# Attention output made as column pairs in the gate/up stage instead of as single sets in the down stage

## The chip, the cores and the metric

The kernel runs on one core of one Trainium2 chip. The metric is the device time of one execution in microseconds; quoted is the median of several executions. Ratios are computed as the mean time of one kernel's fast runs over the mean of the other's fast runs of the same rounds, so they are not quite the ratio of the medians quoted beside them (nor, in the main comparison, quite that of the means of the four times listed for each kernel, which is 0.9993 where the record has 0.9989).

## The reference, cut to what matters

```python
xn = layernorm(x)                                  # x: 2048 x 1024
q, k, v = split(xn @ wqkv)                         # 32 heads of 32
pq, pk = phi(q), phi(k)
kv  = einsum("hsd,hse->hde", pk, v);  z = sum_s(pk)
o   = (pq @ kv) / (pq . z + 1e-6)                  # per head
s   = o @ wo
g   = silu( (silu(xn @ w_gate) * (xn @ w_up)) @ w_down )   # hidden width 3584
out = x + s * g
```

The kernel folds `kv` and `wo` into one 1024 x 1024 matrix M, so that `s` = (normalised pq) @ M. It works in two passes of 1024 rows. A pass has a gate/up stage (queries, gate and up projections, hidden blocks kept in SBUF) and a down stage (four column sets; each gives a quarter of the output columns).

## The kernel before: the parts that matter

Every large product is done with a seven-product scheme: a 2 x 2 block product takes 7 block products in place of 8, paid for with sums of blocks on VectorE. In gate/up two column sets form a **pair**, and products 1 and 5 of both sets, which share the moving operand, are done together by the same scheme once more with 256 columns (the *inner* scheme).

The operand order of TensorE is fixed; a planner in the kernel's own Python gives each other engine a fixed order too, by deadlines that it works out from TensorE's order. ScalarE and VectorE then run that order whatever happens.

After the queries of a pass are made, they are normalised. ScalarE scales the broadcast reciprocals by z, VectorE multiplies, and the result goes to DRAM:

```python
def normalise_part(p, j, half):           # four parts for each pass
    ...                                    # four broadcast loads of 128 KB into rb
    for gl in range(4):
        ...
        act([z_r, zrr], [zrr], zr, zr, ACT.Identity, "sb", scale=zc[:, g:g + 1])
        tt([sr, zrr], [sr], dst, src, zr, ALU.mult, True)
    dma([H.reg(o, 4 * KB)], [named("q", p, half, j)], q_scr[p, half, j], ...)
```

In the down stage the queries come back into X and each of the four sets does 14-matmul products D1 to D7 (down projection) and 4-matmul products S1 to S7 (attention), both with 512 columns:

```python
feed(None)
pq_load(p)                                 # 4 loads of 512 KB, then the four query combinations
for c in range(4):
    Sx = wd_load(c);  ms = m_load(c);  d_set(p, c, Sx, ms)
# inside d_set, by set:
seq = ("D1 D5 D6 D2 D7 S1 S5 D3 S2 S6 D4 S7 S3 S4", ...)[min(c, 2)]
xo_ring, pt_ring, t4_ring = rings[link]    # t4_ring: three places of 2 KB for the T4 differences
```

Product D4 needs seven differences T4 = R10 - T2, made by VectorE as they are used.

Of the kernel before, what the change touches and what calls it, by code (L numbers as in the profile page):

```python
# [10 lines left out]
ALU = mybir.AluOpType  # L11
# [209 lines left out]
def build_kernel(nc, A_x, A_wqkv, A_wo, B_w_gate, B_w_up, B_w_down, out, WINDOW=6, NWARM=14, NPE=4, LEAD=12.0):  # L221
# [12 lines left out]
    with ExitStack() as es:  # L234
# [44 lines left out]
        m_v = m_scr.rearrange("(g p) c -> p g c", p=128)  # L279
        q_scr = nc.dram_tensor("q_scratch", [2, 2, 2, 128, 4 * 512], FP16)  # L280
        r_scr = nc.dram_tensor("r_scratch", [2, 2, 32, 512], BF16)
# [134 lines left out]
        rr_ring = Ring(TM, 20 * KB, 2 * KB, 1)  # L416
        fin_ring = Ring(TM, 10 * KB, 1 * KB, 8)
        x_ring = Ring(W, 32 * KB, 2 * KB, 4)
# [21 lines left out]
        XV = [xview(0, X), xview(1, P)]  # L440
        QV = xview(0, X)

# [491 lines left out]

        def wload(src, joint):


            s = raw_ring.take()
            dma([], [s.r], s.ap().rearrange("p (kt n) -> p kt n", n=512), src, dsem("wr%d" % s.k), 1024 * KB)
            v = s.ap().rearrange("p (kt w n) -> p w kt n", w=2, n=256)  # L940
            c = cmb_ring.take()
# [38 lines left out]
        IN_AT = (((W, 48 * KB), (W, 49 * KB), (W, 50 * KB)), ((W, 51 * KB), (TM, 8 * KB), (TM, 9 * KB)))  # L980
        xin = {}

        def x_inner(v):

            for m, at in zip((1, 5), IN_AT):
                ap, r = v[XOF[m]]
                B = {(k, j): ap[:, 2 * k:2 * k + 2, 256 * j:256 * j + 256] for k in range(2) for j in range(2)}
                t = [(a.at(o, KB, FP16).rearrange("p (k t) -> p k t", t=256), a.reg(o, KB)) for a, o in at]
                tt([r], [t[1][1]], t[1][0], B[1, 1], B[0, 1], ALU.subtract, True)
                tt([r], [r], B[0, 1], B[0, 1], B[0, 0], ALU.subtract, True)  # L990
                tt([r], [t[0][1]], t[0][0], B[1, 1], B[0, 1], ALU.subtract, True)
                tt([r, t[0][1]], [t[2][1]], t[2][0], B[1, 0], t[0][0], ALU.subtract, True)
                xin[m] = {1: (B[0, 0], r), 2: (B[1, 0], r), 3: (B[1, 1], r), 5: (B[0, 1], r), 6: t[0], 7: t[1], 4: t[2]}

        def joint_of(jstat, s0, s1):
            def ops(m):
                def f(k):
                    ws, wr = jstat(m, k)
                    xa, xr = xin[m][k]
                    return [(ws[q], xa[:, q, :]) for q in range(2)], [wr, xr]  # L1000
                return f
            return {"1": Joint(ops(1), lambda w, b: (s0, s1)[w].put1(b)),
                    "5": Joint(ops(5), lambda w, b: (s0, s1)[w].put5(b))}
# [17 lines left out]
        def q_load(p, s):  # L1021
            return wload(wqkv_v[:, :, s * 512:(s + 1) * 512], QJ[p][s])

        PQ0 = 52 * KB

# [46 lines left out]

        RB0 = 68 * KB

        def normalise_part(p, j, half):
# [9 lines left out]
            for gl in range(4):  # L1085
# [5 lines left out]
                tt([sr, zrr], [sr], dst, src, zr, ALU.mult, True)  # L1091
            o = PQ0 + (2 * half + j) * 4 * KB
            dma([H.reg(o, 4 * KB)], [named("q", p, half, j)], q_scr[p, half, j], H.at(o, 4 * KB, FP16),
                dsem("pq%d%d" % (half, j)), 512 * KB)

# [56 lines left out]

        def pq_load(p):
            for j in range(2):
                for k in range(2):
                    v, vr = xblock(X, 2 * j + k)
                    dma([named("q", p, k, j)], [vr], v, q_scr[p, k, j].rearrange(
                        "p (g t) -> p g t", t=512), dsem("pql%d%d" % (k, j)), 512 * KB)
            combos(QV)


        GB = 3584

        rings = ((Ring(TM, 18 * KB, 2 * KB, 3), Ring(TM, 24 * KB, 1 * KB, 2),
                  Places([(W, 40 * KB), (W, 42 * KB), (TM, 8 * KB)], 2 * KB)),
                 (Ring(X, 8 * KB, 2 * KB, 3), Ring(X, 14 * KB, 1 * KB, 2),
                  Places([(W, 40 * KB), (W, 42 * KB)], 2 * KB)))
        dd_ring = Ring(TM, 4 * KB, 2 * KB, 2)
        MR, MC = 44 * KB, 48 * KB
        PL_A, PL_B, PL_C, PL_D, PL_E = 8 * KB, 24 * KB, 16 * KB, 32 * KB, 0  # L1170
        RAW_AT = ((PL_A, PL_B), (PL_E, PL_A), (PL_B, PL_E), (PL_A, PL_B))

        def wd_load(c):


            A = {}
            for k in range(2):
                o = RAW_AT[c][k]
                v = W.at(o, 2 * GB).rearrange("p (n q) -> p n q", q=256)
# [17 lines left out]

        def m_load(c):
            raw = W.at(MR, 4 * KB, FP16).rearrange("p (g n) -> p g n", n=256)
            rr = W.reg(MR, 4 * KB)  # L1200
            dma([named("mscr", c // 2)], [rr], raw, m_v[:, :, c * 256:(c + 1) * 256], dsem("mld"), 512 * KB)
            cv = W.at(MC, 4 * KB, FP16).rearrange("p (m kt n) -> p m kt n", m=4, n=128)
            cr = [W.reg(MC + q * KB, KB) for q in range(4)]
            A = {(k, i): raw[:, 4 * k:4 * k + 4, i * 128:i * 128 + 128] for k in range(2) for i in range(2)}
            tt([rr], [cr[0]], cv[:, 0], A[0, 1], A[1, 1], ALU.add, True)
            tt([rr, cr[0]], [cr[1]], cv[:, 1], cv[:, 0], A[0, 0], ALU.subtract, True)
            tt([rr], [cr[2]], cv[:, 2], A[0, 0], A[0, 1], ALU.subtract, True)
            tt([rr, cr[1]], [cr[3]], cv[:, 3], A[1, 0], cv[:, 1], ALU.subtract, True)

            def stat(w, m):  # L1210
                if m in (1, 2, 4):
                    k, i = {1: (0, 0), 2: (1, 0), 4: (1, 1)}[m]
                    return [raw[:, 4 * k + q, i * 128:i * 128 + 128] for q in range(4)], rr
                q4 = {5: 0, 6: 1, 7: 2, 3: 3}[m]
                return [cv[:, q4, q, :] for q in range(4)], cr[q4]
            return stat

        out_evs = []

        def d_set(p, c, Sx, mstat):  # L1220
            gv, sv, xo = {}, {}, {}
            last = (p, c) == (1, 3)
            link = (p, c) == (0, 3)
            xo_ring, pt_ring, t4_ring = rings[link]

            def fin(i, j):
                if (i, j) not in gv or (i, j) not in sv:
                    return
                g, s = gv[i, j], sv[i, j]
                tt([g.r, s.r], [g.r], g.ap(FP16), g.ap(FP16), s.ap(FP16), ALU.mult, True)  # L1230
                row = p * 1024 + j * 512
# [47 lines left out]
            def dops(m):  # L1279
# [17 lines left out]
                for q in range(0, NPAIR, 7):  # L1297
# [3 lines left out]
            dset = Set(dops, keep(gv, ACT.Silu), dd_ring)  # L1301
            sset = xset(mstat, 0, QV, keep(sv, ACT.Identity), dd_ring)
            seq = ("D1 D5 D6 D2 D7 S1 S5 D3 S2 S6 D4 S7 S3 S4", "D1 S1 D5 S5 S2 D6 S6 D2 S7 S3 D7 S4 D3 D4",
                   "S1 S5 S2 S6 D1 S7 S3 D5 S4 D6 D2 D7 D3 D4")[min(c, 2)]
            if link:
                seq = "S1 S5 S2 S6 D1 S7 S3 D5 S4 X D6 nj1a D2 nj1b D7 nj1c D3 nj1d nj5a D4 nj5b n2_0 nj5c n6_0 n2_1 nj5d n6_1"
                nxt = None
            for w in seq.split():
                if w == "X":
                    nxt = turn_pass()  # L1310
                elif w[0] == "n":
                    nxt.do(w[1:])
                else:
                    (dset if w[0] == "D" else sset).step(int(w[1]))
                    tick()
# [4 lines left out]
        combos(XV[0])  # L1320
        order = [("q", 0), ("g", 0), ("u", 0), ("q", 1)] + [(k, n) for n in range(1, NPAIR // 2) for k in "gu"]
        lq = deque([(k, p, n) for p in range(2) for k, n in order])
        got = {}
        gate = [0]

        def pump(n):
            while lq and len(got) < n and lq[0][1] <= gate[0]:
                k, p, s = lq.popleft()
                got[k, p, s] = q_load(p, s) if k == "q" else gu_load(k, s)

# [10 lines left out]
        def turn_pass():  # L1341
# [3 lines left out]
            gate[0] = 1  # L1345
            raw_ring.__init__([(W, o * KB) for o in (0, 16, 8)], 8 * KB)
            cmb_ring.__init__([(X, 0), (W, 24 * KB), (W, 32 * KB)], 8 * KB)
            in_ring.__init__([(W, o * KB) for o in (44, 46, 40, 42)], 2 * KB)
# [5 lines left out]
        for p in range(2):  # L1354
            for k, n in order:
# [8 lines left out]
                if n == 2:  # L1364
                    at = {w: [partial(normalise_part, p, "gu".index(k), h)] for h, w in enumerate(("2_1", "7_1"))}
                if last_pair[0] is not None and (p, k, n) == (1, "q", 0):
                    pass
                elif k == "q":
                    q_pair(p, n, st, at)
                else:  # L1370
                    gu_pair(p, k, n, st, at)
# [3 lines left out]
            feed(None)  # L1375
            pq_load(p)
            for c in range(4):
                Sx = wd_load(c)
                ms = m_load(c)
                d_set(p, c, Sx, ms)  # L1380
        flush()
# [68 lines left out]
```

## Time and profile before

| kernel before | value |
|---|---|
| time, median of 4 | 731.58 us (731.53 to 733.25) |
| TensorE busy, profiled execution | 717.3 of 731.5 us |
| VectorE, ScalarE busy | 596.5 us, 397.7 us |
| matmuls | 3894 |

The lines that carry this are in the prediction below.

For comparing traces I use one derived quantity, the **loss** of TensorE: for each matmul, the distance to the next start less what a matmul of its width takes undisturbed (215.7 ns at 512 columns, 109.2 ns at 256; the few other shapes with the distance that they usually show). The sum of the undisturbed distances is the ideal time.

### The profile page before, as it was taken

How to read it: one execution, taken by the hardware profiler on the slowest of the kernel's cores; microseconds unless marked ns; L12 is line 12 of the kernel's file. 1: busy time of each engine (PE TensorE's matmuls, PEld its weight loads, DVE VectorE, ACT ScalarE, POOL GpSimd, SP SyncE). 2: the span in 40 equal slices, each digit the busy share in tenths (PEclk: the TensorE clock that was granted, in tenths of full speed). 3: DMA queues.
4: the chain of work that ended last, by engine and by line, in shares of the span. 5: the costliest groups of instructions: out<-in, count | busy, mean ns of one | idle time of the engine just before them, and what ended most of it. 6: DMA issues, size and time to landing. Idle time of an engine off the chain costs nothing.

```text
span 731.5 us, 10526 instructions
## 1 busy us (share of the span) xinstructions
PE 717.3 (98%) x3894; PEld 365.9 (50%) x3894; DVE 596.5 (82%) x1395; ACT 397.7 (54%) x743; POOL 14.1 (2%) x35
## 2 busy tenths in 40 slices
PE   8999999999999999999999999999999999999996
PEld 3444445455555555544444455555455554444442
DVE  6999868979989998787457889999899988757353
ACT  3776654787659766623232376767786654223231
POOL 2111000000000000000000000000000000000000
PEclk9999999999999999999999999999999999999999
DMA  9443235135257432471846534132835245274822
GB/s 293 110 102 86 44 111 176 59 109 166 75 149 217 156 109 65 130 216 32 213 118 153 170 86 152 59 116 76 245 145 173 74 136 167 77 166 118 177 65 50
DMA packets 135219, 94.00 MB, mean 129 GB/s; under 512 B 32512, under 2 KB 131072, under 8 KB 135168
## 3 DMA queue, kind: packets, MB, share of 16 engines
q1 hardware_dynamic: 135168, 93.34, 44.9%
q8 instruction: 30, 0.49, 0.3%
q14 instruction: 21, 0.17, 0.1%
HBM read 75.50 MB, written 10.62 MB: 118 GB/s over the span
## 4 chain that ended last, share of the span: by engine, by line
PE 86%; DVE 6%; ACT 4%; DMA 2%; issue 1%; POOL 0%; SPq 0%; ACTq 0%; DVEq 0%
PE ps L210 86%; ACT TM L341 2%; ACT H L341 2%; DMA W<-in_B_w_up_dram 1%; DVE H L717 1%; DVE W L348 1%; DVE ps L348 1%; DVE stats L642 1%; DVE TM L348 1%; DVE H L348 1%; ACT L341 1%; DVE TM L716 0%; DVE stats L646 0%; DMA W<-in_A_x_dram 0%; ACT ps L341 0%
## 5 line engine op out<-in xcount | busy, mean ns | idle before, releaser
L210 PE MATMUL ps<-X,W 128*128 128x512 f16 (+1 forms) x1408 | 312.0, 361 | 0.9 <-DVE ps L348 0.5
L341 ACT ACTIVATE TM<-ps 128x512 f16<-128x512 f32 (+2 forms) x337 | 181.7, 556 | 152.6 <-PE ps L210 148.5
L210 PE MATMUL ps<-H,W 128*128 128x512 f16 (+1 forms) x896 | 206.8, 379 | 0.3 <-DVE ps L348 0.3
L210 PEld LDWEIGHTS ps<-X,W 128*128 128x128 f16 (+1 forms) x1408 | 136.6, 98 | 122.2 <-DVE ps L348 2.3
L348 DVE TENSOR_TENSOR W<-W 128x256 f16<-128x256 f16 (+6 forms) x424 | 169.1, 440 | 9.7 <-DMA W<-in_B_w_down_dram 5.7
L348 DVE TENSOR_TENSOR ps<-ps,TM 128x256 f32<-128x256 f32 (+1 forms) x218 | 117.1, 540 | 33.1 <-PE ps L210 32.2
L210 PEld LDWEIGHTS ps<-H,W 128*128 128x128 f16 (+1 forms) x896 | 87.2, 98 | 103.4 <-DVE ps L348 0.7
L341 ACT ACTIVATE ps<-ps 128x512 f32<-128x512 f32 (+1 forms) x156 | 78.6, 504 | 59.3 <-PE ps L210 55.6
L341 ACT ACTIVATE H<-ps 128x512 f16<-128x512 f32 (+1 forms) x126 | 74.9, 602 | 57.4 <-PE ps L210 57.2
L210 PE MATMUL ps<-P,W 128*128 128x256 f16 (+1 forms) x440 | 90.0, 323 | 0.1
L210 PE MATMUL ps<-W 128*128 128x256 f16 (+1 forms) x328 | 69.7, 299 | 2.2 <-DVE ps L348 1.7
L348 DVE TENSOR_TENSOR TM<-ps,TM 128x512 f32<-128x512 f32 (+1 forms) x60 | 40.8, 681 | 29.4 <-PE ps L210 28.8
L341 ACT ACTIVATE TM<-TM 128x512 f16<-128x512 f32 (+1 forms) x61 | 37.9, 621 | 44.1 <-DVE TM L348 43.6
L210 PEld LDWEIGHTS ps<-P,W 128*128 128x128 f16 (+1 forms) x440 | 42.9, 98 | 32.9 <-DVE H L717 0.5
L348 DVE TENSOR_TENSOR H<-H,TM 128x512 f16<-128x512 f16 x112 | 45.2, 417 | 12.7 <-ACT H L341 12.4
L348 DVE TENSOR_TENSOR H<-H 128x1024 f16<-128x1024 f16 (+2 forms) x82 | 50.5, 629 | 0.6 <-DMA H<-in_A_wqkv_dram 0.3
L210 PEld LDWEIGHTS ps<-W 128*128 128x128 f16 (+1 forms) x328 | 30.8, 98 | 27.9 <-DVE ps L348 3.5
L348 DVE TENSOR_TENSOR TM<-TM 128x512 f16<-128x512 f16 (+1 forms) x59 | 24.2, 419 | 18.3 <-DMA TM<-TM 10.7
L210 PE MATMUL ps<-H,X 128*128 128x512 bf16 (+1 forms) x136 | 32.2, 379 | 1.2 <-ACT X L341 0.8
L210 PE MATMUL ps<-TM,W 128*128 128x256 f16 (+1 forms) x144 | 30.9, 296 | 0.3 <-DVE ps L348 0.3
L348 DVE TENSOR_TENSOR W<-H 128x1024 f16<-128x1024 f16 x40 | 26.9, 685 | 3.0 <-PE ps L210 2.8
L716 DVE TENSOR_SCALAR TM<-TM 128x512 f16<-128x512 f16 x64 | 17.7, 285 | 10.3 <-ACT TM L341 10.1
(81 smaller groups left out, 413.1 us busy)
## 6 DMA issues: line engine op xcount, KB each, us to landing
W<-in_B_w_gate_dram SPq DMA_DIRECT2D x14, 1024.0 KB, 5.3
W<-in_B_w_up_dram SPq DMA_DIRECT2D x14, 1024.0 KB, 5.5
W<-in_B_w_down_dram SPq DMA_DIRECT2D x16, 896.0 KB, 6.1
W<-in_A_x_dram SPq DMA_DIRECT2D x16, 256.0 KB, 3.0
H<-in_A_wqkv_dram SPq DMA_DIRECT2D x8, 512.0 KB, 8.3
W<-in_A_wqkv_dram SPq DMA_DIRECT2D x4, 1024.0 KB, 5.2
H<-r_scratch SPq DMA_DIRECT2D x32, 128.0 KB, 4.0
q_scratch<-H SPq DMA_DIRECT2D x8, 512.0 KB, 4.0
```

Of the source, the lines that this page charges most:

```text
L210: last = h.matmul(o, l, r, start=st, stop=sp, skip_group_check=True)
L341: return PL.op("act", reads, writes, lambda h: h.activation(o, i, func, **kw), nel(o) / 1200.0 + (0.055 if src == "ps" else 0.095))
L348: return dve(reads, writes, lambda h: h.tensor_tensor(o, a, b, op), nel(o), 1.92 if fast else 0.96)
L642: o0 = dve([s.r], [sA], lambda h: h.bn_stats(stats[:, j, 0, :], xa[:, 0:512]), 512)
L716: dve([e.r], [b.r], lambda h: h.tensor_scalar(ba, ea, 1.0, EPS_PHI, ALU.min, ALU.add), 512, 2.6)
L717: dve([src_r, b.r], [out_r], lambda h: h.scalar_tensor_tensor(out_ap, src, 0.0, ba, ALU.max, ALU.add), 512)
```

## The change

The attention output of a pass is made in the gate/up stage, after the eighth of the gate and up pairs, as two pairs in the style of the gate pairs (inner scheme included), straight from the queries in SBUF. The results wait in DRAM until the down stage multiplies them in. The down sets keep only D1 to D7. Memory places are dealt out anew, and in the second pass T4 gets eight places instead of three. The core of the diff, cuts marked:

```diff
-        q_scr = nc.dram_tensor("q_scratch", [2, 2, 2, 128, 4 * 512], FP16)
+        s_scr = nc.dram_tensor("s_scratch", [2, 4, 2, 128, 2 * 512], FP16)
 ...
-            o = PQ0 + (2 * half + j) * 4 * KB
-            dma([H.reg(o, 4 * KB)], [named("q", p, half, j)], q_scr[p, half, j], ...)
 ...
-        def pq_load(p): ...
+        def s_load(n):
+            return wload(m_v[:, :, n * 512:(n + 1) * 512], (1, 5), FP16, [named("mscr", n)])
+        def s_pair(p, n, stats, at):
+            def evac(w):
+                def f(i, j, ap, r, bank):
+                    o = st_ring.take()                       # four places of 1 KB
+                    act([r], [o.r], o.ap(FP16), ap, ACT.Identity, ...)
+                    dma([o.r], [named("s", p, 2 * n + w, i)], s_scr[...], ..., 128 * KB)
+            s0, s1 = (xset(stat, w, QV, evac(w), d_ring) for w in range(2))
+            feed(Pair(s0, s1, joint_of(jstat, s0, s1, qin), at))
 ...
+        t4_late = Ring(P, 0, 2 * KB, 8)
 ...
-            seq = ("D1 D5 D6 D2 D7 S1 S5 D3 S2 S6 D4 S7 S3 S4", ...)[min(c, 2)]
+            seq = "1 5 6 2 7 3 4"
 ...
+        order[10:10] = [("s", 0), ("s", 1)]
 ...
+                if (k, n) == ("g", 3):
+                    at = {"2_1": [partial(combos, QV)], "7_1": [partial(x_inner, QV, qin, QIN_AT)]}
```

More of the change, by code (lines that the diff above doesn't have):

```diff
@@ L416, in build_kernel @@
         rr_ring = Ring(TM, 20 * KB, 2 * KB, 1)
-        fin_ring = Ring(TM, 10 * KB, 1 * KB, 8)
+        fin_ring = Ring(TM, 10 * KB, 1 * KB, 6)
         x_ring = Ring(W, 32 * KB, 2 * KB, 4)
@@ L440, in build_kernel, with hblock @@
         XV = [xview(0, X), xview(1, P)]
-        QV = xview(0, X)
+        def hblock(o):
+            return H.at(o, 4 * KB, FP16).rearrange("p (k t) -> p k t", t=512), H.reg(o, 4 * KB)
+        PQ0, RB0 = 52 * KB, 68 * KB
+        QV = {nm: hblock(o) for nm, o in (("R00", PQ0), ("T1", PQ0 + 4 * KB), ("R01", PQ0 + 4 * KB),
+                                          ("R10", PQ0 + 8 * KB), ("R11", PQ0 + 12 * KB), ("T2", RB0),
+                                          ("T3", RB0 + 4 * KB), ("T4", RB0 + 8 * KB))}
         def combos(v):
@@ L933, in build_kernel, with wload @@
         SUM_OF = {5: 0, 6: 1, 7: 2, 3: 3}
-        def wload(src, joint):
+        def wload(src, joint, dt=BF16, rd=()):
             s = raw_ring.take()
-            dma([], [s.r], s.ap().rearrange("p (kt n) -> p kt n", n=512), src, dsem("wr%d" % s.k), 1024 * KB)
-            v = s.ap().rearrange("p (kt w n) -> p w kt n", w=2, n=256)
+            dma(list(rd), [s.r], s.ap(dt).rearrange("p (kt n) -> p kt n", n=512), src, dsem("wr%d" % s.k), 1024 * KB)
+            v = s.ap(dt).rearrange("p (kt w n) -> p w kt n", w=2, n=256)
             c = cmb_ring.take()
@@ L980, in build_kernel, with x_inner @@
         IN_AT = (((W, 48 * KB), (W, 49 * KB), (W, 50 * KB)), ((W, 51 * KB), (TM, 8 * KB), (TM, 9 * KB)))
-        xin = {}
-        def x_inner(v):
-            for m, at in zip((1, 5), IN_AT):
+        QIN_AT = (((H, 80 * KB), (H, 81 * KB), (H, 82 * KB)), ((H, 83 * KB), (H, 48 * KB), (H, 49 * KB)))
+        xin, qin = {}, {}
+        def x_inner(v, xin=xin, places=IN_AT):
+            for m, at in zip((1, 5), places):
                 ap, r = v[XOF[m]]
@@ L993, in x_inner, with joint_of @@
                 xin[m] = {1: (B[0, 0], r), 2: (B[1, 0], r), 3: (B[1, 1], r), 5: (B[0, 1], r), 6: t[0], 7: t[1], 4: t[2]}
-        def joint_of(jstat, s0, s1):
+        def joint_of(jstat, s0, s1, xin=xin):
             def ops(m):
@@ L1022, in q_load @@
             return wload(wqkv_v[:, :, s * 512:(s + 1) * 512], QJ[p][s])
-        PQ0 = 52 * KB
         def pq_tile(g, j):
@@ L1071, in recip @@
                 o0 = o0 or o1
-        RB0 = 68 * KB
         def normalise_part(p, j, half):
@@ L1091, in normalise_part @@
                 tt([sr, zrr], [sr], dst, src, zr, ALU.mult, True)
-            o = PQ0 + (2 * half + j) * 4 * KB
-            dma([H.reg(o, 4 * KB)], [named("q", p, half, j)], q_scr[p, half, j], H.at(o, 4 * KB, FP16),
-                dsem("pq%d%d" % (half, j)), 512 * KB)
         HB = 6 * KB
@@ L1150, in h_sums @@
             tt([v["R11"][1], v["T1"][1]], [v["T2"][1]], v["T2"][0], v["R11"][0], v["T1"][0], ALU.subtract, True)
-        def pq_load(p):
-            for j in range(2):
-                for k in range(2):
-                    v, vr = xblock(X, 2 * j + k)
-                    dma([named("q", p, k, j)], [vr], v, q_scr[p, k, j].rearrange(
-                        "p (g t) -> p g t", t=512), dsem("pql%d%d" % (k, j)), 512 * KB)
-            combos(QV)
+        def s_load(n):
+            return wload(m_v[:, :, n * 512:(n + 1) * 512], (1, 5), FP16, [named("mscr", n)])
@@ new lines, in build_kernel @@
+        st_ring = Places([(TM, o * KB) for o in (20, 24, 21, 25)], KB)
+        def s_pair(p, n, stats, at):
+            stat, jstat = stats
+            def evac(w):
+                def f(i, j, ap, r, bank):
+                    o = st_ring.take()
+                    act([r], [o.r], o.ap(FP16), ap, ACT.Identity, "ps" if bank is not None else "sb")
+                    dma([o.r], [named("s", p, 2 * n + w, i)], s_scr[p, 2 * n + w, i, :, j * 512:j * 512 + 512],
+                        o.ap(FP16), dsem("ss%d" % o.k), 128 * KB)
+                return f
+            s0, s1 = (xset(stat, w, QV, evac(w), d_ring) for w in range(2))
+            feed(Pair(s0, s1, joint_of(jstat, s0, s1, qin), at))
@@ L1162, in build_kernel @@
         GB = 3584
-        rings = ((Ring(TM, 18 * KB, 2 * KB, 3), Ring(TM, 24 * KB, 1 * KB, 2),
+        rings = ((Places([(TM, o * KB) for o in (22, 18, 20)], 2 * KB), Ring(TM, 24 * KB, 1 * KB, 2),
                   Places([(W, 40 * KB), (W, 42 * KB), (TM, 8 * KB)], 2 * KB)),
-                 (Ring(X, 8 * KB, 2 * KB, 3), Ring(X, 14 * KB, 1 * KB, 2),
+                 (Ring(X, 8 * KB, 2 * KB, 2), Ring(X, 12 * KB, 1 * KB, 2),
                   Places([(W, 40 * KB), (W, 42 * KB)], 2 * KB)))
+        t4_late = Ring(P, 0, 2 * KB, 8)
@@ L1168, in build_kernel @@
         dd_ring = Ring(TM, 4 * KB, 2 * KB, 2)
-        MR, MC = 44 * KB, 48 * KB
-        PL_A, PL_B, PL_C, PL_D, PL_E = 8 * KB, 24 * KB, 16 * KB, 32 * KB, 0
-        RAW_AT = ((PL_A, PL_B), (PL_E, PL_A), (PL_B, PL_E), (PL_A, PL_B))
-        def wd_load(c):
+        S_AT = tuple(((W, o * KB), (W, o * KB + 2 * KB)) for o in (44, 48)) + (((X, 16 * KB), (X, 18 * KB)),)
+        S_LINK = ((X, 14 * KB), (TM, 16 * KB))
+        PL_C, PL_D = 24 * KB, 32 * KB
+        RAW3 = ((0, 8 * KB, 16 * KB), (16 * KB, 0, 8 * KB))
@@ L1176, in wd_load @@
+        def wd_load(p, c):
             A = {}
             for k in range(2):
-                o = RAW_AT[c][k]
+                o = RAW3[p][(2 * c + k) % 3]
                 v = W.at(o, 2 * GB).rearrange("p (n q) -> p n q", q=256)
@@ L1196, in wd_load, with s_fetch, d_set @@
             return Sx
-        def m_load(c):
-            raw = W.at(MR, 4 * KB, FP16).rearrange("p (g n) -> p g n", n=256)
-            rr = W.reg(MR, 4 * KB)
-            dma([named("mscr", c // 2)], [rr], raw, m_v[:, :, c * 256:(c + 1) * 256], dsem("mld"), 512 * KB)
-            cv = W.at(MC, 4 * KB, FP16).rearrange("p (m kt n) -> p m kt n", m=4, n=128)
-            cr = [W.reg(MC + q * KB, KB) for q in range(4)]
-            A = {(k, i): raw[:, 4 * k:4 * k + 4, i * 128:i * 128 + 128] for k in range(2) for i in range(2)}
-            tt([rr], [cr[0]], cv[:, 0], A[0, 1], A[1, 1], ALU.add, True)
-            tt([rr, cr[0]], [cr[1]], cv[:, 1], cv[:, 0], A[0, 0], ALU.subtract, True)
-            tt([rr], [cr[2]], cv[:, 2], A[0, 0], A[0, 1], ALU.subtract, True)
-            tt([rr, cr[1]], [cr[3]], cv[:, 3], A[1, 0], cv[:, 1], ALU.subtract, True)
-            def stat(w, m):
-                if m in (1, 2, 4):
-                    k, i = {1: (0, 0), 2: (1, 0), 4: (1, 1)}[m]
-                    return [raw[:, 4 * k + q, i * 128:i * 128 + 128] for q in range(4)], rr
-                q4 = {5: 0, 6: 1, 7: 2, 3: 3}[m]
-                return [cv[:, q4, q, :] for q in range(4)], cr[q4]
-            return stat
+        def s_fetch(p, c):
+            got = []
+            for i, (ar, o) in enumerate(S_LINK if (p, c) == (0, 3) else S_AT[c % 3]):
+                r = ar.reg(o, 2 * KB)
+                dma([named("s", p, c, i)], [r], ar.at(o, 2 * KB, FP16), s_scr[p, c, i], dsem("sl%d%d" % (c % 3, i)),
+                    256 * KB)
+                got.append((ar.at(o, 2 * KB, FP16), r))
+            return got
         out_evs = []
-        def d_set(p, c, Sx, mstat):
-            gv, sv, xo = {}, {}, {}
+        def d_set(p, c, Sx, sv):
+            gv, xo = {}, {}
             last = (p, c) == (1, 3)
@@ L1224, in d_set @@
             xo_ring, pt_ring, t4_ring = rings[link]
+            if p == 1:
+                t4_ring = t4_late
             def fin(i, j):
-                if (i, j) not in gv or (i, j) not in sv:
-                    return
-                g, s = gv[i, j], sv[i, j]
-                tt([g.r, s.r], [g.r], g.ap(FP16), g.ap(FP16), s.ap(FP16), ALU.mult, True)
+                g, (sa, sr) = gv[i, j], sv[i]
+                tt([g.r, sr], [g.r], g.ap(FP16), g.ap(FP16), sa[:, j * 512:j * 512 + 512], ALU.mult, True)
                 row = p * 1024 + j * 512
@@ L1301, in d_set @@
             dset = Set(dops, keep(gv, ACT.Silu), dd_ring)
-            sset = xset(mstat, 0, QV, keep(sv, ACT.Identity), dd_ring)
-            seq = ("D1 D5 D6 D2 D7 S1 S5 D3 S2 S6 D4 S7 S3 S4", "D1 S1 D5 S5 S2 D6 S6 D2 S7 S3 D7 S4 D3 D4",
-                   "S1 S5 S2 S6 D1 S7 S3 D5 S4 D6 D2 D7 D3 D4")[min(c, 2)]
+            seq = "1 5 6 2 7 3 4"
             if link:
-                seq = "S1 S5 S2 S6 D1 S7 S3 D5 S4 X D6 nj1a D2 nj1b D7 nj1c D3 nj1d nj5a D4 nj5b n2_0 nj5c n6_0 n2_1 nj5d n6_1"
+                seq = "1 5 X 6 nj1a 2 nj1b 7 nj1c 3 nj1d nj5a 4 nj5b n2_0 nj5c n6_0 n2_1 nj5d n6_1"
                 nxt = None
@@ L1313, in d_set @@
                 else:
-                    (dset if w[0] == "D" else sset).step(int(w[1]))
+                    dset.step(int(w))
                     tick()
@@ L1328, in pump @@
                 k, p, s = lq.popleft()
-                got[k, p, s] = q_load(p, s) if k == "q" else gu_load(k, s)
+                got[k, p, s] = q_load(p, s) if k == "q" else s_load(s) if k == "s" else gu_load(k, s)
         pump(2)
@@ L1345, in turn_pass @@
             gate[0] = 1
-            raw_ring.__init__([(W, o * KB) for o in (0, 16, 8)], 8 * KB)
-            cmb_ring.__init__([(X, 0), (W, 24 * KB), (W, 32 * KB)], 8 * KB)
+            raw_ring.__init__([(X, 0), (W, 0), (W, 8 * KB)], 8 * KB)
+            cmb_ring.__init__([(W, o * KB) for o in (16, 24, 32)], 8 * KB)
             in_ring.__init__([(W, o * KB) for o in (44, 46, 40, 42)], 2 * KB)
@@ L1369, in build_kernel @@
                     q_pair(p, n, st, at)
+                elif k == "s":
+                    s_pair(p, n, st, at)
                 else:
@@ L1375, in build_kernel @@
             feed(None)
-            pq_load(p)
             for c in range(4):
-                Sx = wd_load(c)
-                ms = m_load(c)
-                d_set(p, c, Sx, ms)
+                Sx = wd_load(p, c)
+                d_set(p, c, Sx, s_fetch(p, c))
         flush()
```

## The prediction

> **What bounds the kernel now.** I read the page from the top. Its first part names the engine, the chain of work shows whether that engine also sets the end, and the stretches tell where another engine comes close.
>
> ```profile
> span 731.5 us, 10526 instructions
> ...
> PE 717.3 (98%) x3894; PEld 365.9 (50%) x3894; DVE 596.5 (82%) x1395; ACT 397.7 (54%) x743; POOL 14.1 (2%) x35
> ...
> PE 86%; DVE 6%; ACT 4%; DMA 2%; issue 1%; POOL 0%; SPq 0%; ACTq 0%; DVEq 0%
> ```
>
> TensorE is busy for 717.3 of 731.5 us, and the chain that ends last runs through its matmuls for 86% of the span. All idle time of TensorE together is 14.2 us, so what the change can win by removing waits is at most that, and most of it lies in the start and the tail, which the change doesn't touch. Everything else has to come from fewer matmul columns. The wait list of TensorE (releaser, then us in total, times, longest) holds only small sums:
>
> ```profile
> PE ps L210 <- DVE ps L348: 3.0, 6, 1.3
> PE ps L210 <- POOL ident L391: 1.4, 1, 1.4
> PE ps L210 <- ACT TM L341: 1.3, 1, 1.3
> PE ps L217 <- DVE TM L348: 1.1, 1, 1.1
> ```
>
> Then I need the true price of a matmul, which is not the 379 ns mean duration that the groups print (matmuls overlap in the pipe) but the distance between starts. In the timeline of TensorE I take these lines (start, us, what):
>
> ```profile
> 644.64 3.19 PE L210 MATMUL ps<-H,W 128*128 128x512 f16 x14
> 647.66 1.03 PE L210 MATMUL ps<-X,W 128*128 128x512 f16 x4
> ...
> 265.47 0.38 PE L210 MATMUL ps<-W 128*128 128x256 f16 x2
> 265.69 1.25 PE L210 MATMUL ps<-X,W 128*128 128x256 f16 x6
> ...
> 277.16 0.38 PE L210 MATMUL ps<-W 128*128 128x256 f16 x2
> ```
>
> Fourteen matmuls of 512 columns take 647.66 - 644.64 = 3.02 us: **215.7 ns each**. Two of 256 columns take 265.69 - 265.47 = 0.22 us, about 109 ns each. The check is a whole gate/up pair, which repeats after 277.16 - 265.47 = 11.69 us and by the code holds 40 of the large and 28 of the small ones: (11.69 - 40 x 0.2157) / 28 = **109.4 ns**. Both the gate/up and the down stage run at that pace, with a granted clock of 1.00.
>
> Last, who else is near full? The stretches (VectorE and ScalarE busy per stretch; TensorE first) of two places in gate/up and one in the down stage:
>
> ```profile
> 222.00:234.00 12.00, 11.88 (x70) 6.43 (x69) 11.90 (x32) 11.78 (x25) 0.00 (x0) 1.00 0.83 243
> 282.00:294.00 12.00, 12.00 (x71) 6.78 (x70) 10.05 (x26) 7.03 (x15) 0.00 (x0) 1.00 0.29 89
> 353.00:380.00 27.00, 27.00 (x127) 12.25 (x126) 17.26 (x35) 8.32 (x14) 0.00 (x0) 1.00 0.55 141
> ```
>
> In 222 to 234 us, where the queries are normalised, both VectorE and ScalarE are full; later in gate/up VectorE is at 84%; in the down stage it has a third of its time free. **The change moves work from the stage with slack to the stage without.** That is the whole risk.
>
> **What the Trainium skill says.** "TensorE: Matmul & The Clock Gate", section "Wait — 56ns, not 53.3ns?", gives start to start N / 2.4 GHz plus about 2.5 ns when warm, 215.7 ns at 512 columns; for 256 this makes 109.2 ns. The trace agrees: 215.7 and 109.4. So halving the columns costs about one fixed 2.5 ns more and no more. "VectorE: DVE Perf Modes", section "The perf-mode tier table", lets a two-tensor operation on 16-bit SBUF data run at 2x and drops it to 1x with an operand in PSUM. The trace agrees: 128x1024 f16 sums in SBUF show 682 ns and 128x512 f32 sums on PSUM 690 ns, half the elements for the same time. "DMA: Bandwidth & Descriptors", section "Anatomy of one DMA", puts a fixed 2 us or so on a transfer (for another issuing path); here 128 KB stores of the same kind (m_scratch) land in 1.8 us, so a ring of four staging places should do.
>
> **The change part by part.**
> 1. *Matmuls.* Attention output (pq times M) is now made for each half of the rows as 8 column blocks in the down stage: 4 sets per pass, 7 products of 4 large matmuls each, 2 x 4 x 28 = 224 matmuls, 224 x 0.2157 = 48.3 us. After the change two sets form a pair: 5 products of each set stay (40 large), products 1 and 5 of both sets together become 7 inner products of 2 matmuls of 256 columns (28 small). A pair is 11.69 us as the gate/up pairs show; 4 pairs are 46.8 us. **Gain 1.6 us** (8 inner savings of one eighth: 4 x (56 x 0.2157 - 11.69) = 1.57). All of it on TensorE, hence on the path. The number of matmuls rises by 4 x 68 - 224 = 48.
> 2. *Tail.* In the last set product 4 needs seven differences T4 made by VectorE into three places. In the trace 12 of its 14 matmuls take from 721.70 to 725.22, 3.52 us, where 12 x 0.2157 = 2.59: 0.9 us lost, VectorE (0.60 us between two differences) being slower than two matmuls (0.43 us) and too few places letting it run ahead. The change gives the second pass eight places in the then free P region, so all seven can be ready. **Gain 0.9 us**, on the path.
> 3. *Query round trip.* 8 stores and 8 loads of 512 KB go; 32 stores of 128 KB and 16 loads of 256 KB of results come: 4 MB each way before and after. Loads of M: 8 of 512 KB become 4 of 1 MB. Bytes are even and DMA is mostly under half busy: worth 0 by itself. But in the second pass TensorE lost 1.33 us at 522.97, and the chain shows a weight load of 9.9 us (511.74 on, usual 5.5) behind broadcast loads and a query store there. With the stores gone perhaps **0.5 us** comes back.
> 4. *VectorE and ScalarE in gate/up.* Added per pass there: two pairs' ordinary work, each 4 sums of about 0.60 us, 8 inner sums of 0.20, 4 joint adds of 0.34, 4 set adds of 0.60 = 7.7 us in 11.7, light beside a gate pair with the same and an up pair with some 4.5 us more. Moved in front of them: the four query combinations, 4 x 1.13 = 4.5 us (1.22 us each in the trace, less overlap), and the new inner ones, 8 x 0.34 = 2.7 us. These must be ready when the first pair begins, about where the trace has 242 us, and before them the normalisation, 16 ScalarE scalings of 0.66 us and 16 VectorE products of 0.34 us, now finished near 244 us as filler. Between about 206 and 242 us VectorE has some 11 us of such filler or idle time (5.4 products, 3.6 hidden-block sums that may go later, 2.2 idle); what is then needed is 5.4 + 4.5 + 2.7 = 12.6, of which 2.3 us (the T2 and T4 combinations) can wait into the first pair. So it just about fits. I allow **1.0 us lost** over both passes.
> 5. *Down stage and the link to pass two.* Without the attention sets a down set is 98 x 0.2157 = 21.1 us instead of 27.2 us. Evictions hide behind 14-matmul products (3.0 us against about 0.7 us each). In the link the combinations for the second half now have 21 us instead of 27; in the trace TensorE already loses some 1.1 us to VectorE in 432 to 444. I allow **0.2 us** more.
>
> Sum: 731.6 - 1.6 - 0.9 - 0.5 + 1.0 + 0.2 = **729.8 us**.
>
> **The rivals.**
> - *VectorE becomes the bound in gate/up.* For it: 11.9 of 12 us busy from 222 to 234, and a backlog worked off until about 260 us in the trace. Against it: instructions are ordered by deadline, the normalisation was late because nobody needed it, and the S pairs with 7.7 us in 11.7 give relief right after. If the operands come 2 us late in each pass: 732 to 735 us.
> - *The link starves.* X is free earlier (no queries in it), which lets two of the four combinations start in the set before; yet if they don't, TensorE waits 2 to 3 us at about 410 us less the shift: 732 us.
> - *All waits in gate/up vanish as well* (both losses around 520 to 535 us, about 2 us): 727.5 us.
> - *The transfers matter.* Four staging places for results of 0.5 us each with a store near 2 us: in bursts of six tiles ScalarE could wait on a store. PSUM has other banks free, so I expect under 0.5 us.
>
> **Range and chances.** The gains of 2.5 us are well founded; the rest is give and take of -2 to +4 us. Range 727.2 to 733.2. Two per cent are 14.6 us, which no rival reaches: within 2% 0.97, slower 0.02, faster 0.01.
>
> **What would show it.** TensorE: 3942 matmuls (3894 + 48, some records may be missing), busy time down by about 1.6 us. Two more pairs of 11.7 us before the fourth gate pair's follower, with VectorE full in the 30 us before them and perhaps gaps of up to 1 us at their first inner products. Down sets of 21.1 us with no gaps between. The last product 4 with 2.6 us for twelve matmuls. If the time rises, look for gaps released by VectorE at the first attention pair of each pass or after the link; if I am wrong by much, a weight load or an M load came late in a ring that now turns differently.

## More of the kernel before

At the very end SyncE waits for every DMA semaphore in the order in which they were first used:

```python
for s in semn.values():
    if id(s) in PL.count:
        prog["sp"].append(("w", s, PL.count[id(s)]))
```

The times of the first batch are 733.25, 731.59, 731.53 and 731.56 us.

## The result, and the profile after

The changed kernel takes **731.33 us** (731.14 to 731.96, 4 runs) against 731.58 us; the ratio is 0.9989, 95% interval 0.9972 to 1.0005. That is the same within 2%, inside the range 727.2 to 733.2, and 1.5 us above the point of 729.8.

The head of the page after; the third line is the chain of work by engine:

```profile
span 729.5 us, 10728 instructions
...
PE 715.9 (98%) x3942; PEld 371.1 (51%) x3942; DVE 612.8 (84%) x1443; ACT 400.5 (55%) x759; POOL 14.1 (2%) x35
...
PE 85%; ACT 7%; DVE 5%; issue 2%; POOL 0%; ACTq 0%; DVEq 0%; POOLq 0%
```

The matmul count is 3942, as worked out. The chain now holds 7% of ScalarE where it held 4%. VectorE works 16 us more over the whole program and ScalarE 3 us.

The wait list of TensorE after (releaser, us in total, times, longest), the lines that differ:

```profile
PE ps L210 <- ACT TM L341: 1.7, 2, 1.3
...
PE ps L210 <- DVE ps L348: 1.4, 5, 0.4
...
PE ps L210 <- ACT ps L341: 0.8, 3, 0.3
```

By the second profile of the kernel before (first experiment) VectorE's line was 1.7 us, and ScalarE's were 1.3 and 0.3 us. So VectorE holds TensorE up a little less, and ScalarE some 0.9 us more. (The 3.0 us for VectorE in the prediction include the 1.3 us gap of the slower execution.)

**The tail.** First the timeline of TensorE before, then after, at the last product 4:

```profile
721.70 1.03 PE L210 MATMUL ps<-W 128*128 128x512 f16 x4
722.56 0.59 PE L210 MATMUL ps<-TM,W 128*128 128x512 f16 x2
723.08 0.61 PE L210 MATMUL ps<-W 128*128 128x512 f16 x2
724.02 0.60 PE L210 MATMUL ps<-W 128*128 128x512 f16 x2 [0.33 <-DVE W L348]
```

```profile
718.91 1.67 PE L210 MATMUL ps<-H,W 128*128 128x512 f16 x7
720.42 2.75 PE L210 MATMUL ps<-P,W 128*128 128x512 f16 x12
```

Before, pairs of matmuls start 0.5 to 0.9 us apart because VectorE delivers one T4 at a time; after, the last twelve run in one piece of 2.75 us, reading from P.

**The stretch before the first attention pair.** The stretches after (TensorE busy first, then weight loads, VectorE, ScalarE):

```profile
220.00:232.00 12.00, 11.79 (x69) 6.35 (x67) 11.49 (x31) 12.00 (x24) 0.00 (x0) 1.00 0.74 182
232.00:244.00 12.00, 11.64 (x66) 5.99 (x64) 11.75 (x27) 10.86 (x23) 0.00 (x0) 1.00 0.27 88
```

ScalarE is busy for the whole of the first stretch. Its timeline shows with what: first the kernel after, then the kernel before (its second profile, see the first experiment) over the same 15 us. The H<-H,zc lines are the scalings of the normalisation:

```profile
226.54 3.19 ACT L341 ACTIVATE H<-H,zc 128x512 bf16<-128x512 bf16 x5
229.60 0.40 ACT L341 ACTIVATE ps<-ps 128x256 f32<-128x256 f32 x1
...
233.56 2.58 ACT L341 ACTIVATE H<-H,zc 128x512 bf16<-128x512 bf16 x4
236.00 1.10 ACT L341 ACTIVATE TM<-ps 128x512 f16<-128x512 f32 x2
```

```profile
226.35 2.58 ACT L341 ACTIVATE H<-H,zc 128x512 bf16<-128x512 bf16 x4
...
232.79 1.33 ACT L341 ACTIVATE H<-H,zc 128x512 bf16<-128x512 bf16 x2
...
236.90 1.37 ACT L341 ACTIVATE H<-H,zc 128x512 bf16<-128x512 bf16 x2
```

Before, one burst of four stands at 226 us, and from 230 us on the scalings go two at a time between evictions; after, a burst of five and one of four stand ahead of evictions that TensorE waits for. Its timeline after shows the largest stops and who released each (the idle time in brackets is shorter than the loss, which is 0.38, 0.45 and 0.43 us here):

```profile
230.06 0.39 PE L210 MATMUL ps<-X,W 128*128 128x256 f16 x2 [0.21 <-ACT ps L341]
...
237.65 4.49 PE L210 MATMUL ps<-X,W 128*128 128x512 f16 x20 [0.29 <-ACT ps L341]
...
244.58 1.05 PE L210 MATMUL ps<-H,W 128*128 128x256 f16 x8 [0.27 <-DVE ps L348]
```

A stop like the first, of 0.28 us, was there before too. The third is in the inner products of the first attention pair and is put down to VectorE. The chain of work after runs through just these pieces (start, us, what):

```profile
226.54 3.19 ACT H L341 x5
229.73 0.27 ACT ps L341
230.01 0.78 ACT TM L341 x2
...
233.67 2.46 ACT H L341 x4
```

A chain names one way through, not the only one, since VectorE is nearly as full. It is a suspicion so far; the experiments test it.

### The profile page after: what moved, and what is told of

Read it like the earlier page. It is cut to its first block, busy times and chain, and to the rows that moved or that the text cites. A ratio compares the mean times of both kernels' runs of the same rounds, so it can differ in the third digit from the quotient of the medians.

```text
span 729.5 us, 10728 instructions
## 1 busy us (share of the span) xinstructions
PE 715.9 (98%) x3942; PEld 371.1 (51%) x3942; DVE 612.8 (84%) x1443; ACT 400.5 (55%) x759; POOL 14.1 (2%) x35
## 4 chain that ended last, share of the span: by engine, by line
PE 85%; ACT 7%; DVE 5%; issue 2%; POOL 0%; ACTq 0%; DVEq 0%; POOLq 0%
PE ps L210 85%; ACT H L341 3%; ACT TM L341 2%; DVE W L348 2%; DVE H L348 1%; DVE TM L348 1%; ACT ps L341 1%; DVE ps L348 1%; ACT L341 1%; DVE stats L649 0%; DVE stats L653 0%; DVE TM L724 0%; PE ps L217 0%; DVE X L348 0%; POOL rstd L658 0%
## 5 line engine op out<-in xcount | busy, mean ns | idle before, releaser
L210 PE MATMUL ps<-X,W 128*128 128x512 f16 (+1 forms) x1232 | 268.0, 358 | 1.1 <-ACT ps L341 0.5
L210 PE MATMUL ps<-H,W 128*128 128x512 f16 (+2 forms) x1168 | 256.4, 369 | 0.5 <-DVE ps L348 0.5
L348 DVE TENSOR_TENSOR W<-W 128x256 f16<-128x256 f16 (+5 forms) x440 | 176.4, 437 | 7.2 <-DMA W<-in_B_w_down_dram 7.0
L210 PEld LDWEIGHTS ps<-H,W 128*128 128x128 f16 (+1 forms) x1168 | 113.5, 98 | 124.1 <-DVE ps L348 2.3
L210 PEld LDWEIGHTS ps<-X,W 128*128 128x128 f16 (+1 forms) x1232 | 119.3, 98 | 102.8 <-ACT ps L341 2.2
L210 PE MATMUL ps<-P,W 128*128 128x512 f16 (+1 forms) x496 | 104.7, 329 | 0.7 <-ACT TM L341 0.4
L348 DVE TENSOR_TENSOR H<-H 128x1024 f16<-128x1024 f16 (+4 forms) x106 | 66.1, 640 | 1.0 <-ACT H L341 0.5
L210 PE MATMUL ps<-W 128*128 128x256 f16 (+1 forms) x278 | 56.5, 289 | 0.6 <-DVE ps L348 0.4
L348 DVE TENSOR_TENSOR P<-H 128x1024 f16<-128x1024 f16 x28 | 19.0, 686 | 9.2 <-PE ps L210 9.2
L348 DVE TENSOR_TENSOR H<-ps,TM 128x512 f16<-128x512 f32 (+1 forms) x35 | 23.9, 682 | 2.3 <-PE ps L210 1.7
```

What stands on the lines that cost most here:

```text
L210: last = h.matmul(o, l, r, start=st, stop=sp, skip_group_check=True)
L348: return dve(reads, writes, lambda h: h.tensor_tensor(o, a, b, op), nel(o), 1.92 if fast else 0.96)
```

## The experiments

Three batches of four kernels, each batch on one chip with runs of the kernel before in between. The before medians of the batches are 731.91, 732.48 and 732.92 us, so times of different batches are compared by their ratios or by their traces, not by medians. The changed kernel was not run again in them.

**1. The kernel before again.** No edit. Is the 1.5 us gap at 521 us in the first profile part of the kernel?

> The kernel before, unchanged, profiled a second time. Theory A: its first profile caught an execution of 733.25 us, 1.7 us over its median, and the 1.5 us gap of TensorE at 521 us (a late weight load) is of that execution alone; then this profile shows a span near 729.8 us and a loss of TensorE between 510 and 540 us of about 0.8 us instead of 2.3. Rival B: the gap is of the kernel; then the span is 731.5 us again and the loss 2.3 us. Time 731.6 us either way.

Median 732.54 us, ratio 1.0011 (0.9993 to 1.003). The span of this profile is 729.8 us and the loss between 505 and 545 us is 0.86 us, where the first profile has 2.29. Theory A holds. The weight load that was late, as the transfers by line show it in 505 to 530 us, first profile, second profile, and the changed kernel:

```profile
W<-in_B_w_up_dram SPq DMA_DIRECT2D x1, 1024.0 KB, 9.9
```

```profile
W<-in_B_w_up_dram SPq DMA_DIRECT2D x1, 1024.0 KB, 7.6
```

```profile
X<-in_B_w_up_dram SPq DMA_DIRECT2D x1, 1024.0 KB, 5.9
```

In the kernel before all 16 broadcast loads of the reciprocals are issued around this load; in the changed one eight go out 9 us before it, because the queries are needed sooner. The kernel before's executions in this batch lie at 731.5 to 732.3 us or at 733.0 to 733.6 us, apart from one of 736.29; none of the changed kernel's four goes above 731.96, and of the six variants of it in experiments 3 to 8 no one's executions lie more than 0.9 us apart. That the slower ones are those with the late load is shown for the profiled execution only. Why the same order of transfers took 9.9 us once and 7.6 us once stays open.

**2. and 3. The eight places alone, and the change without them.** In the kernel before:

```diff
+        t4_late = Ring(P, 0, 2 * KB, 8)
 ...
             xo_ring, pt_ring, t4_ring = rings[link]
+            if p == 1:
+                t4_ring = t4_late
```

> The kernel before with only the eight places for T4 in the second pass's down stage. Theory A: the last product 4 runs without its 0.9 us of gaps, time 730.6 to 730.8 us. Rival: the tail is set by the evictions and stores behind it, time 731.5 us unchanged.

Median 731.62 us, ratio 0.9989 (0.9977 to 1.0001). And the same `if` taken out of the changed kernel:

> The changed kernel without the eight places. Theory A: 0.9 us slower than the changed kernel, 732.2 us, with gaps between the matmuls of the last product 4. Rival: unchanged at 731.3 us.

Median 732.18 us, ratio 0.9999 (0.9986 to 1.0012). The losses after 700 us come straight from the traces: 2.27 us in the kernel before, 1.32 with the eight places; 1.32 us in the changed kernel, 2.09 without them. So this part is worth 0.95 us in the one and 0.77 in the other, and **it doesn't need the attention pairs at all**. The changed kernel without it is not measurably faster than the kernel before, and the kernel before with it has the ratio of the whole change, 0.9989.

**4. Attention pairs one gate pair later.** The queries lie where the up pair after that writes its hidden blocks, so later is not possible.

```diff
-        order[10:10] = [("s", 0), ("s", 1)]
+        order[11:11] = [("s", 0), ("s", 1)]
```

> The changed kernel with the two attention pairs one gate pair later, after the fifth gate pair and before its up pair, so the normalisation and the sums before the pairs get 11.7 us more. Theory A (VectorE and ScalarE are overfull from 220 to 250 us because the pairs need them by then): the loss of TensorE in that stretch falls from 1.7 to 0.4 us and the second pass's from 1.1 to about 0.5; time 729.5 us. Rival (the loss is there whatever the deadline, since the same work runs): 731.3 us, the loss only moves.

Median 730.37 us, ratio 0.9974 (0.9962 to 0.9986). The loss from 200 to 260 us falls from 1.74 to 0.94 us (expected 0.4), from 505 to 545 us from 1.13 to 0.93 (expected 0.5). The direction is right, but of the falls of 1.3 and 0.6 us that were expected 0.8 and 0.2 us came: with more time less is lost, but what causes the loss is still there.

**5. Broadcast loads 12 us earlier.**

```diff
+                o0.urgent = 12.0
                 first = first or o0
```

> The changed kernel with the broadcast loads of the reciprocals asked for 12 us earlier, so that ScalarE's 16 scalings can use its idle time from 205 to 220 us. Theory S (ScalarE's scalings stand before its evictions from 220 to 240 us and hold TensorE up): the loss from 220 to 250 us falls from 1.7 to under 0.8 us, time 730.3 us. Rival V (VectorE has too much to do before the first attention pair whatever the order): loss stays at 1.5 us or more, 731.3 us. Rival D: the earlier loads meet a weight load and make it late: slower, 732 us, with gaps behind a weight load.

Median 730.7 us, ratio 0.9973 (0.9961 to 0.9986), but not for the expected reason. By the trace eight of the pass's sixteen loads moved, from 214 to 204 us. From 220 to 250 us the loss is 0.38 us, under the expected 0.8, but from 200 to 260 us it is 1.93 us where the changed kernel has 1.74. It moved. TensorE now stops for 1.0 us at 218.3 us, again behind ScalarE, where the new timeline has the scalings in bursts of two and four from 214 us. So in this run the loss moved with the bursts. Of the better time, 0.4 us is in the closing waits (from the last data moved to the end: 1.62 us against 2.01), which this edit doesn't touch: a stop of 0.37 us, which the next experiment shows, is missing. The profiled span is only 0.3 us shorter than the changed kernel's; what the ratio shows beyond that isn't explained.

**6. Closing waits in another order.** The trace of SyncE after the last store, from its records (start in us, waits for). The kernel before (second profile):

```
728.784 semaphore 163      <- store has landed
728.843 semaphore 164      ... nine more, about 60 ns apart
729.394 branch             729.739 end
```

and after:

```
727.905 semaphore 160      <- store has landed
727.967 semaphore 161      ... thirteen more, 60 ns apart but for one stop of 0.37 us before the last
729.139 branch             729.480 end
```

From landing to the end it is 0.95 us before and 1.57 us after. The whole list has hardly grown (69 DMA semaphores before, 70 after), but four that fetch results stand behind the output store's, 13 instead of 9: that is 0.24 us. The other 0.37 us is the one stop, whose cause no run shows. The edit:

```diff
-        for s in semn.values():
+        for nm, s in sorted(semn.items(), key=lambda kv: kv[0].startswith("oo")):
```

> The changed kernel with the closing waits of SyncE in another order: the semaphores of the output stores last, all others before. Theory E (after the last store has landed, SyncE still works through the 13 waits that follow it in the list at 60 ns each, with one stop of 0.4 us, 1.57 us from landing to the end against 0.95 us in the kernel before): the stretch from landing to the end shrinks to about 0.6 us, time 730.3 us. Rival: the last store itself takes the time: 731.3 us unchanged.

Median 730.75 us, ratio 0.9975 (0.9961 to 0.9988). From the last data moved to the end it is now 1.40 us, against 2.01 in the changed kernel and 1.36 before. Theory E holds with 0.6 us, for ten waits fewer behind the store; the 1 us that it hoped for included the stop, which is still there. The profiled execution was the slowest of its five, with 0.5 us lost at the start, so that its span is the changed kernel's 729.5 us.

**7. Attention pairs without the inner scheme.**

```diff
-            return wload(m_v[:, :, n * 512:(n + 1) * 512], (1, 5), FP16, ...)
+            return wload(m_v[:, :, n * 512:(n + 1) * 512], (), FP16, ...)
-            feed(Pair(s0, s1, joint_of(jstat, s0, s1, qin), at))
+            feed(Pair(s0, s1, None, at))
-                    at = {"2_1": ..., "7_1": [partial(x_inner, QV, qin, QIN_AT)]}
+                    at = {"2_1": ...}
```

> The changed kernel with the attention pairs made without the inner scheme: two plain sets of 28 large matmuls, no inner sums, no joint products. Matmul work rises by 1.6 us. If the losses before and around the pairs come from the sums for the inner scheme (2.7 us of VectorE per pass for the queries, 1.6 for each M pair, joint adds 1.3), they fall by about 0.5 us per pass and the time is 732 us; if not, 732.9 us; more if a plain pair, which is not interleaved with its predecessor, exposes evictions.

Median 731.25 us, ratio 0.9981 (0.9968 to 0.9993): by ratio and span (729.7 against 729.5 us) as fast as the changed kernel, though with 1.6 us more of matmuls. The loss from 200 to 260 us is 0.39 us instead of 1.74, from 505 to 545 us 0.93 instead of 1.13. At this place **the inner scheme earns nothing**. Why isn't settled by this run: it removes sums from VectorE, but a plain pair is also not interleaved with the pair ahead of it, so that its operands are needed some 6 us later (an estimate, half a pair of 11.7 us).

**8. Later pairs and reordered waits together.** Both edits.

> Later attention pairs and the reordered closing waits together, on the changed kernel. If the two effects are independent: 730.4 - 1.0 = 729.4 us, a span of 727.6 us, 2.2 us under the kernel before. If the closing waits only hide other work: 730.4 us.

Median **729.85 us** (729.68 to 729.95), ratio 0.9962 (0.9949 to 0.9974): the fastest correct kernel. The sum of the two effects would have been 729.4 us. In the trace both are there in full: 0.93 us of loss from 200 to 260 us, and 0.6 us less from the last data to the end.

**9. No scalings.** Wrong result (relative error 0.97): ScalarE's line is taken out, VectorE's work is left as it is.

```diff
-                act([z_r, zrr], [zrr], zr, zr, ACT.Identity, "sb", scale=zc[:, g:g + 1])
```

> The changed kernel without ScalarE's 32 scalings of the normalisation (wrong result on purpose): 10.6 us of ScalarE less per pass, VectorE's work the same. Theory S (the bursts of scalings on the in-order ScalarE hold up the evictions): the loss of TensorE from 200 to 260 us falls from 1.7 to under 0.5 us and from 505 to 545 us from 1.1 to under 0.4; time 729.3 us. Rival V (VectorE's sums for the inner scheme are the cause): the loss stays above 1.3 us in the first pass; time 731 us.

Median 729.31 us, ratio 0.9946 (0.9928 to 0.9963). The loss from 200 to 260 us is 0.30 us, and from 505 to 545 us 0.00. The stretches of this run:

```profile
220.00:232.00 12.00, 12.00 (x72) 6.72 (x71) 11.79 (x33) 7.74 (x17) 0.00 (x0) 1.00 0.80 207
232.00:244.00 12.00, 11.98 (x68) 6.39 (x67) 12.00 (x29) 7.07 (x15) 0.00 (x0) 1.00 0.26 89
```

VectorE is as full as ever, 11.79 and 12.00 of 12 us, and TensorE hardly stops. This decides between the two: **what is too much is ScalarE's scalings, not VectorE's load**. The sums for the inner scheme are all in this run and cost next to nothing once ScalarE has room. What the run doesn't separate is how the scalings do it: by standing ahead of evictions, as the stops at 230 and 237 us say, or also by making VectorE's products late, as the stop at 244.58 us may say. It removes the scalings' cost to the kernel before as well (0.38 and 0.86 us of loss), so it is a bound and not the cost of the change.

**10. Scalings on GpSimd.**

```diff
-                act([z_r, zrr], [zrr], zr, zr, ACT.Identity, "sb", scale=zc[:, g:g + 1])
+                pool([z_r, zrr], [zrr], lambda h, zr=zr, g=g: h.tensor_scalar(
+                    zr, zr, zc[:, g:g + 1], None, ALU.mult), 1.0)
```

> The changed kernel with the 32 scalings on GpSimd, which is idle there. Theory S: as without the scalings if GpSimd needs about 1 us for each and disturbs nobody: loss under 0.6 and 0.5 us, time 729.6 us. Rival: GpSimd is so slow or slows VectorE so much that the queries come late: 732 us or more, with a gap before the first attention pair.

Median 747.07 us, ratio 1.0186 (1.0163 to 1.0209). The rival holds. The groups by line: GpSimd's scalings; then VectorE's two-input products in 221 to 243 us with it, and, in the last fence, in the changed kernel:

```profile
L1094 POOL TENSOR_SCALAR H<-H,zc 128x512 bf16<-128x512 bf16 x32 | 54.2, 1713 | 411.6 <-DMA H<-r_scratch 411.6
```

```profile
L348 DVE TENSOR_TENSOR H<-H 128x512 f16<-128x512 bf16 x13 | 7.9, 611 | 2.4 <-POOL H L1094 2.4
L348 DVE TENSOR_TENSOR ps<-ps,TM 128x256 f32<-128x256 f32 x6 | 2.5, 419 | 0.0
```

```profile
L348 DVE TENSOR_TENSOR H<-H 128x512 f16<-128x512 bf16 x16 | 6.3, 417 | 0.3 <-ACT H L341 0.3
L348 DVE TENSOR_TENSOR ps<-ps,TM 128x256 f32<-128x256 f32 x6 | 2.6, 426 | 0.4 <-PE ps L210 0.4
```

GpSimd needs 1.7 us for what ScalarE does in 0.74, and while it works VectorE's products of two SBUF operands take 611 ns instead of 417; those with one operand in PSUM don't change (419 and 426). The Trainium skill, "SBUF — State Buffer", section "Who interferes with whom", says so: a VectorE instruction with two SBUF inputs contends with a GpSimd one that reads SBUF. The trace agrees for the products, though the 128x1024 sums in the same window stayed at 678 ns. VectorE also stood idle for GpSimd, 4.1 us from 205 to 270 us, since in its fixed order it waits for the scaled reciprocals. So the slow scalings and the slower products both delay it, and this run doesn't say which costs more. TensorE's wait list shows the result:

```profile
PE ps L210 <- DVE ps L348: 13.4, 16, 2.3
```

**11. What the kernel before gains without the pairs.** The eight places and the reordered waits on it.

> The kernel before with the two things that do not need the attention pairs: eight places for T4 and the output stores' semaphores waited for last. If the attention pairs themselves gain nothing net, this is as fast as the changed kernel with its waits reordered or faster: 730.2 us against 730.7. If the pairs do gain, it is slower than that: 731.2 us or more.

Median 731.34 us (730.41 to 733.11), ratio 0.9979 (0.9958 to 1.0000). By ratio that is level with the changed kernel with its waits reordered (0.9975). Its span of 728.9 us is 0.6 us shorter than that one's 729.5, of which 0.5 us is the slow start named there. The medians that were expected can't decide, since this batch's kernel before is 1 us slower than the first's, and the interval is too wide to rank the two. So it is not shown that the attention pairs by themselves gain anything as they stand. Later pairs (0.9962) look better than either, but the intervals touch.

**12. Later pairs, GpSimd and reordered waits.**

> Later pairs, scalings on GpSimd and the reordered waits together on the changed kernel. If the losses add up as measured singly: 729.85 us less the remaining 0.9 + 0.6 us of loss in the two normalisation stretches, 728.6 us. If GpSimd disturbs: 730 us or more.

Median 743.87 us, ratio 1.0144 (1.0121 to 1.0166). Here too the rival: TensorE loses 7.6 and 7.5 us in the two normalisation stretches. Of the second, 1.6 us is not waiting: after an idle time of 2.7 us the matmuls run at twice their usual distance from 532.1 to 535.5 us, and the granted clock of 532 to 535.5 us is 0.52. More time before the pairs doesn't mend it.

## Why the prediction was right, and where its steps were off

The range held and the class was right, but the class was no test: by the prediction's own count no rival reached 2%. The point was 1.5 us low, and the way from 731.58 to 731.33 us can be told from traces: the second profile of the kernel before (span 729.79 us) against the changed kernel's (729.53 us), both of executions at their kernel's usual time.

| term | predicted | measured |
|---|---|---|
| matmul columns (ideal sum 708.34 to 706.75 us) | -1.6 | -1.59 |
| tail, T4 places (loss after 700 us: 2.27 to 1.32) | -0.9 | -0.95 |
| late weight load in pass two | -0.5 | 0 in the usual execution |
| gate/up, around the pairs (200-260, 505-545 and 545-700 us: 0.38, 0.86, 0.01 to 1.74, 1.13, 0.16) | +1.0 | +1.78 |
| link to pass two (400-450 us: 2.09 to 1.70) | +0.2 | -0.39 |
| closing waits (last data to end: 1.36 to 2.01) | not in it | +0.65 |
| start and the rest | 0 | +0.24 |
| sum | -1.8 | -0.26 |

(The second profile lacks 14 matmul records, all before 200 us; the ideal sum is therefore taken from the first profile, and the start is the rest to the span.)

- *What bounds the kernel* was right, and so were steps 1 and 2, to the tenth of a microsecond: they rested on start distances and on counts from the code. (Its opening remark that the change doesn't touch the tail contradicts step 2.)
- *Step 3* took a gap from one profile as the kernel's. The profiled execution was 1.7 us slower than the median that the sum began with, so 0.5 us was claimed from a gap which that median doesn't hold. The change does remove the late load; in the profiled pair that is worth the 1.5 us at 521 us, but it seems to show in the spread of the times and not in the median.
- *Step 4* is the term that was mis-sized: it allowed 1.0 us and it was 1.8. It also named the wrong engine for most of it: the stop at the first attention pair that it foretold behind VectorE came, with 0.43 us, but the larger part is behind ScalarE. Its balance of "filler" was drawn up for VectorE, while the run without scalings shows that VectorE can be full at almost no cost and that ScalarE's scalings are what costs. ScalarE's 10.7 us of scalings for each pass were not in the balance. The stretch that the prediction quotes had ScalarE at 11.78 of 12 us beside VectorE's 11.90; ScalarE was the tight one. That the bursts arise because the planner books 0.52 us for a scaling which, in a burst, starts every 0.61 us, was not tested.
- *Step 5* had the sign wrong by a little: the link loses less than before.
- *One reading of a page* goes further than the trace. That a VectorE operation drops to 1x with an operand in PSUM is not shown by sums that are f32: the addition at the very end, 16-bit with one operand in PSUM, took 425 ns, hardly more than the 417 ns of such products in SBUF. No step rests on it.
- *Not foreseen* was the end. Four more closing waits came to stand behind the last store (0.24 us), and a stop of 0.37 us appeared among them; no view of the page lists them.

Of the rivals, none came true as written: VectorE was not the bound, the link didn't starve, the gate/up waits didn't vanish. The four staging places for results gave no gap that I found, though their stores took 2.8 us to land (median) and not the 1.8 us that the prediction went by.

So where did the expected 1.8 us go? The 2.5 us of real gain are there. 1.8 us were given back in gate/up, most of it to ScalarE, 0.65 to the closing waits, and 0.5 had never been in the median.

## What to carry to other kernels

Before you take a gap from a profile, check that the profiled execution has the time of the median, and profile the kernel before a second time when the matter is under a per cent. Where two engines are full, take the load off one of them in an experiment before you name the culprit; an engine can be full and cost next to nothing. A part of a change that stands alone (here the T4 places) should be measured alone: they account for all that this change gained net, as far as these runs can tell.

## What the Trainium skill lacked or had wrong

- No page says that the order of a kernel's closing semaphore waits bears on its time: on SyncE each satisfied wait took about 60 ns here, and moving the output stores' to the end of the list was worth 0.6 us (1.40 against 2.01 us from the last data to the end). It would belong to "Perfetto Trace Analysis".
- "SBUF — State Buffer", section "Who interferes with whom", states the contention between GpSimd and VectorE but gives no size for this pair of instructions: 128x512 16-bit products of two SBUF operands rose from 417 to 611 ns on average beside GpSimd scalings of 128x512 bf16, which took 1713 ns each, while the 128x1024 sums in the same window did not rise (678 ns).
- "VectorE: DVE Perf Modes", section "The perf-mode tier table", which the prediction cites, has `tensor_tensor` at 1x with any PSUM operand. Here that fits the f32 sums on PSUM only: the one 128x512 addition that reads f16 from PSUM took 425 ns before and 424 ns after.
